# Spectral mixing and hash-routed experts: the loads of token blocks from the second on, issued by SyncE instead of ScalarE

## The chip, the cores and the metric

The kernel runs on one core of a Trainium2 chip. The metric is the device time of one execution in microseconds (us). The kernel before the change has a median of 1469.29 us over 14 runs (1464.46 to 1480.11). The engines are called PE (TensorE), DVE (VectorE), ACT (ScalarE), POOL (GpSimd) and SP (SyncE). SP does no arithmetic here: it loads registers and issues transfers. ACT copies and applies relu, and issues transfers as well.

## What is computed

The reference, cut to what matters:

```python
# x (8, 2496, 256); filt_r, filt_i (1249, 256)
X = np.fft.rfft(x, axis=1)
Y = X * (filt_r + 1j * filt_i)[None]
y = np.fft.irfft(Y, n=2496, axis=1).reshape(19968, 256)

expert = token_ids * 2654435761 % 8
for e in range(8):
    m = expert == e
    out[m] = np.maximum(y[m] @ w1[e], 0) @ w2[e]      # w1 (8, 256, 1024), w2 (8, 1024, 256)
```

Each of 8 batches goes through a filter in the frequency domain along its 2496 tokens. Then each of the 19968 tokens goes through the two-layer network of one of 8 experts, which its id chooses. All is in 32-bit floats.

## The kernel before

**The spectral part** splits 2496 into 39 x 64 and does each transform as two rounds of small matmuls with table matrices. For a batch there are four kinds of matmuls on PE: `pa` (first round forward, from tiles `x`), `pb` (second round forward, from `t2`, that is slots of the tile `mid`), then the product with the filter on DVE, `pc` (first round back) and `pd` (second round back, from tiles `t`). For batches 2 to 7 the turn of the data between two rounds goes through DRAM: ACT copies the result of `pa` and writes it to `d1` (L286, shown as `d<-mid`), SP reads it as `mid<-d` (L292, `load2`); ACT copies the result of `pc` and writes `d2` (L331, `d<-mid` too), SP reads it as `t<-d` (L395, `load4`). SP also loads the input (`x<-in_x_dram`, L239, `load1`). The finished rows, with their token number in column 256, are scattered by POOL (L414) to a DRAM table `xs`, in which all tokens of an expert lie together, in blocks of 256 rows.

**The expert part** is a loop of steps, one for each block of 256 rows of `xs`; 80 blocks are always worked, and up to 5 more under conditions. Step i is made of:

- `up(i)` (L850): the first layer, as seven products on halves of the matrices instead of eight, into the banks `up_a`, `up_b`, `up_c`. ACT copies the first product out (L861), DVE adds the others to it (L857, `plus`), ACT applies relu (L854). POOL prepares the sums of weights (`tw`, L840) for the step after, DVE the sums of tokens (`st`, L831).
- `down(i)` (L885): the second layer into `dps`; DVE copies it out (L890), POOL scatters the rows to the output (L977).
- From step 50 on `both(i)` takes the place of the two, with seven products in the second layer too (L907 and L912; the sums of `w2` for it, `t2s`, are prepared once and loaded by SP, L450).

**The loads of a step.** The two weight matrices (1 MB each) of block i + 2 are loaded by SP, L445 and L448, into the tile `wts`, which holds two pairs. They wait until PE has done with the pair of block i; when block i + 2 has the same expert as block i the issue is skipped. A block of tokens is loaded by `load(i)` (L807): four transfers of 64 rows each into the tile `xg` (two buffers), laid out so that DVE can transpose 32 x 32 squares (L818, `token_parts`), and one transfer of the 256 token numbers into the tile `no` (eight buffers). These five issues are what the change touches. Before, those of block 0 are shared (three by SP, two by ACT), those of block 1 are SP's, and those of all later blocks are ACT's.

**Where a block is asked for.** `ask(i)` calls `load` for the next block. In `up(i)` it stands after ACT's copy L861 (`between`), where it asks up to block i + 2; at the first quarter of `down(i)` (`spot`, k = 0) it may ask for block i + 3 if that block lies in the same stage as the one before. In `both(i)` it stands after the same copy and asks for block i + 2. A load waits until the transpose of the block two before has freed its buffer.

**Stages.** The spectral work of later batches runs between the steps: `todo` gives each of its pieces a place in units of steps, and `run_until` puts the pieces whose place has come into the program, after `up`, between the quarters of `down`, and after it. The blocks are ordered so that the first ten hold only tokens of batches 0 and 1, the next ten of batches up to 2, and so on (`STAGES = (2, 3, 4, 6, 8)`), so experts start while later batches are still being filtered. The first load of a stage therefore waits for the scatters of the batches that it adds.

**Order and waits.** Each engine works through its instructions in the order of the program; the order is by hand. Waits are put in by the framework. Transfers issued by SP and ACT share eight completion semaphores, and an issue waits until the last transfer that was given its semaphore has landed, whichever engine issued that one.

Of the kernel before, what the change touches and what calls it, by code (L numbers as in the profile page):

```python
# [119 lines left out]
def kernel(  # L120
# [10 lines left out]
    nc = tc.nc  # L131
# [625 lines left out]
    todo += [(-75.5, lambda: [nc.sync.dma_start(out=dram, in_=chip) for dram, chip in put_off])]  # L757
    todo += [(t, lambda k=k: weights(k // 2, k % 2)) for k, t in enumerate((-101, -98, -95, -92))]
    todo += [(-84.9, lambda: begin()), (-84.4, lambda: [load(i) for i in range(2)])]

    def batch(b, t1, t2, t3):
# [36 lines left out]
    def load(i):  # L798

        g = gath.tile([P, TB // 32, C // 4], F32, name=f"xg_{i}", tag="xg")  # L800
        no = nums.tile([P, 2], I32, name=f"no_{i}", tag="no")
        rows = xs[tiles[i] * TB:(tiles[i] + 1) * TB, :]
        moves = [(g[32 * q:32 * q + 32, :, :], rows[:, 64 * q:64 * q + 64].rearrange("(a t) c -> t a c", t=32))
                 for q in range(4)]
        moves.append((no[:].bitcast(F32), rows[:, C:C + 1].rearrange("(h p) c -> p (h c)", p=P)))
        for k, (to, src) in enumerate(moves):
            ld = (nc.sync if i < 2 and (i or k < 3) else nc.scalar).dma_start(out=to, in_=src)  # L807
            for b in range(STAGES[stage_of[i]], B):
                tc.declare_no_dep(ld.ins, group=f"xs_{b}", reason="the tiles of a stage hold tokens of its batches alone")
            if stage_of[i] < G - 1:  # L810
                tc.declare_no_dep(ld.ins, group="xs_pad", reason="places without a token lie in the last stage alone")
            tc.add_to_no_dep_group("xs_read", ld.ins)
        xg[i], to_rows[i] = g, no
# [177 lines left out]
    def ask(i, sooner=False):  # L991

        j = asked[0]
        if j <= i + 2 or (sooner and j == i + 3 < NT and stage_of[j] == stage_of[j - 1]):
            if j < NT:
                load(j)
                asked[0] += 1
# [48 lines left out]
    def rest(k):  # L1046
        with tc.If(used[0] > blocks[k][0]):
            for i in blocks[k]:
                ht = work.tile([P, 2, FP, P], F32, name=f"ht_{i}", tag="ht")
                if i >= NSURE + 2:  # L1050
                    for j in ((i, i + 1) if i == NSURE + 2 else (i + 1,)):
                        if j < NT:
                            load(j)
                    token_parts(i)
                token_sums(i)
                weight_sums(i, nc.vector)
                up(i, ht)
                weights(i + 2, 0)
                down(i, ht)
                store(i)  # L1060
                weights(i + 2, 1)
            if k + 1 < len(blocks):
                rest(k + 1)
# [30 lines left out]
```

## Time and profile before

| | |
|---|---|
| median of 14 runs | 1469.29 us (1464.46 to 1480.11) |
| profiled execution | 1468.48 us, its span 1466.7 us |
| mean granted PE clock | 0.979 |
| PE busy | 1395.8 us, 95% |
| ACT busy | 420.2 us, 29% |
| transfers issued by SP (q1) | 89087 packets, 169.76 MB |
| transfers issued by ACT (q10) | 131806 packets, 56.23 MB |
| transfers issued by POOL (q0) | 19920 packets, 44.59 MB |
| L807 on ACT | 321 issues of `xg`, median 462 ns; 81 of `no`, median 464 ns |
| L807 on SP | 7 issues of `xg`, median 448 ns; 1 of `no`, 452 ns |

Times count from the start of the span. The profile is of one execution, 0.81 us faster than the median of the runs. "Busy" leaves out issuing transfers, loading registers and waiting for semaphores, so ACT's and SP's time in L807 is in none of the shares. `ACTq` and `SPq` name the issue queues of ACT and SP. In a list of waits a line says who waited for whom, then the total in us, how often, and the longest. A wait for several semaphores is put down to the one that came last. Lines of a timeline give start, duration, engine, line of the code, operation, result and source, the number of instructions merged, and in brackets the idle time before with what ended it. The execution falls into three parts: up to about 153 us mostly spectral work and routing, from there to about 1075 us steps 0 to 49 mixed with the spectral work of batches 2 to 7, then steps 50 to 79, which last 12.5 us each.

### The profile page before, as it was taken

Reading aid. Unit: us, or ns where it says so; the run is one execution under the profiler, and the core shown is the slowest. Engines: PE = TensorE matmul, PEld = TensorE weight load, DVE = VectorE, ACT = ScalarE, POOL = GpSimd, SP = SyncE. Lnnn points to the kernel's source line nnn. Section 1 sums busy time; section 2 is a strip of 40 time slices with the busy share of each in tenths; the row PEclk is TensorE's granted clock in tenths of the full one; section 3 lists DMA queues with packets and bytes.
Section 4 is the critical chain, followed back from the end, with each engine's and each line's share of the span. In section 5 each row is a group of like instructions: output and inputs, shape, how many; then the busy total and the mean of one; then the engine's idle time right before and its main releaser. Section 6 shows DMA issues by size and latency. Waiting matters only on the chain.

```text
span 1466.7 us, 26476 instructions
## 1 busy us (share of the span) xinstructions
PE 1395.8 (95%) x9494; PEld 1293.4 (88%) x9494; DVE 871.7 (59%) x1641; ACT 420.2 (29%) x770; POOL 822.7 (56%) x732
## 2 busy tenths in 40 slices
PE   8988799899999989999999899999999999999997
PEld 7976688888988878888999899998999999999997
DVE  7862565366465546533766367744557767677765
ACT  4543122222223213223222222222222222222222
POOL 5066332763465464557535387878855555555553
PEclk9997899999999999999999999999999999999999
DMA  8236675667887597697764667688661616161611
GB/s 234 74 101 216 181 226 156 201 200 240 269 245 245 154 303 229 218 272 242 259 196 120 196 215 233 203 245 244 198 212 43 211 43 209 44 215 45 212 45 34
DMA packets 240947, 272.32 MB, mean 186 GB/s; under 512 B 124940, under 2 KB 210879, under 8 KB 231389
## 3 DMA queue, kind: packets, MB, share of 16 engines
q1 hardware_dynamic: 89087, 169.76, 37.1%
q10 hardware_dynamic: 131806, 56.23, 15.6%
q0 software_dynamic: 19920, 44.59, 8.7%
q8 instruction: 78, 1.28, 0.4%
q14 instruction: 56, 0.46, 0.1%
HBM read 290.24 MB, written 83.53 MB: 255 GB/s over the span
## 4 chain that ended last, share of the span: by engine, by line
PE 80%; DMA 9%; DVE 4%; issue 3%; another core or an unknown queue 1%; ACT 1%; POOL 1%; ACTq 1%; SPq 0%; POOLq 0%; DVEq 0%
PE dps L885 19%; PE up_b L850 8%; PE up_a L850 5%; PE up_c L850 5%; PE pd L257 4%; PE pb L301 4%; PE dnc L912 4%; PE dna L912 4%; PE dnb L912 4%; PE upc L907 4%; PE upa L907 4%; PE pa L257 3%; PE pc L324 3%; PE upe L907 2%; PE upg L907 2%
## 5 line engine op out<-in xcount | busy, mean ns | idle before, releaser
L885 PE MATMUL dps<-wts,ht 128*128 128x256 f32 x1600 | 367.4, 380 | 0.3 <-ACT ht L854 0.3
L885 PEld LDWEIGHTS dps<-wts,ht 128*128 128x128 f32 x1600 | 302.1, 190 | 43.9 <-ACT ht L854 1.3
L977 POOL DMA_INDIRECT out_dram<-osb,no x158 | 165.0, 1045 | 231.4 <-DVE osb L919 142.8
L414 POOL DMA_INDIRECT xs<-o,sidx x176 | 175.9, 1000 | 195.4 <-ACT o L259 78.2
L840 POOL TENSOR_TENSOR tw<-wts 128x512 f32<-128x512 f32 x158 | 204.8, 1297 | 110.7 <-DMA wts<-in_moe_w_dram 81.1
L840 POOL TENSOR_TENSOR tw<-wts,tw 128x512 f32<-128x512 f32 x158 | 205.7, 1302 | 6.2
L857 DVE TENSOR_TENSOR ht<-up_b,ht 128x512 f32<-128x512 f32 x150 | 103.7, 692 | 137.5 <-PE up_b L850 79.0
L854 ACT ACTIVATE ht<-ht 128x512 f32<-128x512 f32 x150 | 94.5, 630 | 201.7 <-DVE ht L857 174.7
L850 PE MATMUL up_a<-xt,wts 128*128 128x128 f32 x800 | 119.1, 283 | 23.8 <-ACT ht L861 11.9
L890 DVE COPY osb<-dps 128x512 f32<-128x512 f32 x50 | 34.6, 692 | 168.0 <-PE dps L885 122.5
L850 PEld LDWEIGHTS up_a<-xt,wts 128*128 128x128 f32 x800 | 108.8, 198 | 28.2 <-ACT ht L861 12.9
L311 DVE TENSOR_TENSOR z<-pb,filt 64x512 f32<-64x512 f32 x160 | 110.2, 689 | 38.0 <-PE pc L324 33.9
L850 PE MATMUL up_b<-st,tw 128*128 128x128 f32 x800 | 110.4, 282 | 4.3 <-DVE ht L857 3.3
L850 PEld LDWEIGHTS up_b<-st,tw 128*128 128x128 f32 x800 | 100.7, 197 | 6.7 <-issue 3.5
L857 DVE TENSOR_TENSOR ht<-up_c,ht 128x512 f32<-128x512 f32 x100 | 69.0, 690 | 46.0 <-PE up_c L850 30.5
L916 ACT ACTIVATE ht<-ht 128x512 f32<-128x512 f32 x90 | 56.8, 631 | 120.5 <-DVE ht L919 72.5
L257 PE MATMUL pd<-t,wi_t 120*117 120x256 f32 x320 | 79.0, 390 | 7.2 <-DVE t L387 5.0
L307 DVE TENSOR_TENSOR y<-pb,filt 128x512 f32<-128x512 f32 x80 | 55.2, 690 | 41.0 <-PE pb L301 26.6
L327 ACT COPY mid<-pc 128x512 f32<-128x512 f32 x60 | 35.0, 584 | 149.7 <-PE pc L324 90.0
L259 ACT COPY o<-pd 117x512 f32<-117x512 f32 x80 | 44.7, 586 | 111.3 <-DMA xg<-xs 41.6
L861 ACT COPY ht<-up_a 128x512 f32<-128x512 f32 x50 | 29.3, 587 | 163.4 <-PE up_a L850 98.7
L257 PEld LDWEIGHTS pd<-t,wi_t 120*117 120x117 f32 x320 | 58.0, 185 | 19.9 <-issue 6.1
(210 smaller groups left out, 2499.1 us busy)
## 6 DMA issues: line engine op xcount, KB each, us to landing
wts<-in_moe_w_dram SPq DMA_DIRECT2D x160, 1024.0 KB
xg<-xs ACTq DMA_DIRECT2D x321, 64.0 KB
mid<-d SPq DMA_DIRECT2D x60, 256.0 KB
d<-mid ACTq DMA_DIRECT2D x60, 256.0 KB
d_t<-t2s SPq DMA_DIRECT2D x15, 1024.0 KB
e_t<-t2s SPq DMA_DIRECT2D x15, 1024.0 KB
t<-d SPq DMA_DIRECT2D x12, 960.0 KB
x<-in_x_dram SPq DMA_DIRECT2D x36, 312.0 KB
```

The source lines that it names most:

```text
L257: nc.tensor.matmul(out=ps[0:cols * H, k, :], lhsT=w[:], rhs=src[:, 2 * i + k, :], start=True, stop=True)
L301: nc.tensor.matmul(out=ps[:, i, :], lhsT=d_t[:, s, :], rhs=rhs, start=True, stop=True)
L311: nc.vector.tensor_tensor(out=z[b], in0=ps[a], in1=f_t[1][64 * hi:64 * hi + 64, s1:s1 + 2, :], op=OP.mult)
L414: st = nc.gpsimd.indirect_dma_start(out=xs[:], out_offset=bass.IndirectOffsetOnAxis(ap=index, axis=0), in_=rows, in_offset=None, bounds_ch ...
L840: eng.tensor_tensor(t[k][:], p, q, op=OP.subtract)
L850: nc.tensor.matmul(out=ps[bank][:, f, :], lhsT=w[:, f * P:(f + 1) * P], rhs=xx, start=first and f == 0, stop=True, skip_group_check=True)
L854: nc.scalar.activation(out=out, in_=in_, func=AF.Relu)
L857: nc.vector.tensor_tensor(out, ps[bank][:], other, op=OP.add)
L885: nc.tensor.matmul(out=ps[:, h, :], lhsT=ht[:, h, fp, :], rhs=w2[:, fp, :], start=(fp == 0), stop=(fp == FP - 1))
L907: nc.tensor.matmul(out=ps[:, f, :], lhsT=w[:, f * P:(f + 1) * P], rhs=xx, start=first and f == 0, stop=True, skip_group_check=True)
L912: nc.tensor.matmul(out=ps[:, 0, :], lhsT=a[:, f, :], rhs=b[:, f, :], start=first and f == 0, stop=True, skip_group_check=True)
L977: st = nc.gpsimd.indirect_dma_start(out=out[:], out_offset=bass.IndirectOffsetOnAxis(ap=to_rows[i][:, h:h + 1], axis=0), in_=o[:, h, :], i ...
```

## The change

One line of `load` is changed:

```diff
         for k, (to, src) in enumerate(moves):
-            ld = (nc.sync if i < 2 and (i or k < 3) else nc.scalar).dma_start(out=to, in_=src)
+            ld = (nc.scalar if i == 0 and k >= 3 else nc.sync).dma_start(out=to, in_=src)
             for b in range(STAGES[stage_of[i]], B):
```

For block 0 the rule gives the same as before (k from 0 to 2 to SP, 3 and 4 to ACT), and for block 1 too (SP). From block 2 on all five transfers are issued by SP. What is transferred, and the place of the call in the program, stay the same; on SP the five issues now stand between the register loads, weights and spectral loads that surround the call. The framework gives the eight semaphores out anew for the changed program. The instructions of PE, DVE and POOL are the same, in the same order; ACT has 166 rows fewer in the list of the built program (956 before, 790 after, alike neighbours counted as one row), SP has 167 more (836 before, 1003 after).

## Prediction

> **What bounds the kernel now.** I read the page first, then the trace by stages, then TensorE's waits inside the stages, then the other engines around the longest waits. The page's span and engine row:
>
> ```profile
> span 1466.7 us, 26476 instructions
> PE 1395.8 (95%) x9494; PEld 1293.4 (88%) x9494; DVE 871.7 (59%) x1641; ACT 420.2 (29%) x770; POOL 822.7 (56%) x732
> ```
>
> PE is the bound: all its idle time is 1466.7 - 1395.8 = 71 us. ACT, from which the change takes work, is busy 29%, so only those of its delays count that reach PE. The table of stretches shows where they are. Its columns are stretch, length, busy us and count of PE, PEld, DVE, ACT and POOL, PE clock, DMA share, GB/s:
>
> ```profile
> 153.00:1075.00 922.00, 885.19 (x5327) 800.37 (x5326) 503.81 (x833) 247.08 (x440) 534.94 (x472) 0.98 0.73 220
> 1075.00:1467.00 392.00, 382.90 (x3394) 381.49 (x3392) 268.73 (x605) 106.24 (x212) 215.16 (x178) 1.00 0.38 115
> ...
> 419.00:426.00 7.00, 5.53 (x32) 5.37 (x33) 2.67 (x4) 2.69 (x6) 5.36 (x6) 0.76 0.90 226
> ...
> 828.00:835.00 7.00, 5.31 (x25) 5.31 (x26) 1.98 (x3) 1.70 (x3) 0.00 (x0) 0.52 0.33 110
> 175.00:183.00 8.00, 4.95 (x12) 3.90 (x13) 3.68 (x7) 1.17 (x2) 5.84 (x5) 0.58 0.44 122
> ```
>
> Up to 153 us the change moves nothing that runs (blocks 0 and 1 keep their engines). From 1075 us on (steps 50 to 79) PE has one wait of 0.6 us. The middle, 153 to 1075, has 922 - 885 = 37 us of PE idle, and after a gap the clock falls to about half for a few us: in the last three rows it is 0.76, 0.52 and 0.58, which is 0.24 x 7 = 1.7, 0.48 x 7 = 3.4 and 0.42 x 8 = 3.4 us lost besides the gap. PE's waits in the middle (total, times, longest):
>
> ```profile
> PE up_a L850 <- ACT ht L861: 11.9, 4, 3.9
> PE up_b L850 <- DVE ht L857: 6.1, 8, 1.9
> PE up_a L850 <- issue: 6.1, 2, 5.7
> PE pa L257 <- DMA x<-in_x_dram: 4.0, 1, 4.0
> PE pd L257 <- DMA t<-d: 2.2, 1, 2.2
> ```
>
> Two of the four waits for ACT's L861 copy come from the issues that the change moves. The larger, on ACT and then on PE:
>
> ```profile
> 817.83 3.99 ACTq L807 DMA_DIRECT2D xg<-xs  x4
> 828.63 0.38 ACTq L807 DMA_DIRECT2D no<-xs  x1
> 829.05 0.59 ACT L861 COPY ht<-up_a 128x512 f32<-128x512 f32 x1 [11.93 <-DMA xg<-xs]
> ```
>
> ```profile
> 829.69 0.58 PE L850 MATMUL up_a<-xt,wts 128*128 128x128 f32 x1 [3.71 <-ACT ht L861]
> ```
>
> Four parts of a block are issued, then ACT stands 6.8 us before the fifth (the numbers, `no`). The trace shows why: SP's and ACT's transfers share eight completion semaphores, and an issue waits until the last transfer on its semaphore has landed. Here that was a `d<-mid` issued at 816.89 and landed at 828.55. The copy that PE needs is queued behind. At 404.4 it is the same: the numbers wait until 418.2 for a 1 MB weight load (issued 403.70, landed 418.23), and PE loses 3.02 us at 420.36.
>
> **The change part by part.**
>
> *Removed from ACT.* Blocks 2 to 81 are loaded: 80 x 5 = 400 issues leave ACT. Their row:
>
> ```profile
> L807 ACTq DMA_DIRECT2D xg<-xs x321: 309/462/2860, 146.1 to 1448.3; - x161
> ```
>
> At a median 0.462 us this is 400 x 0.46 = 185 us of ACT's time; in the middle the 250 issues there hold ACT about 204 us with their waits. Of that only what ends a PE wait counts: 3.71 + 3.4 at 829 and 3.02 + 1.7 at 420, **-11.8 us**. The other two waits for L861 (283.5, 691.3) are not from these issues: ACT stood idle before the copy with nothing of L807 in hand. I leave those, and the 5.7 us "issue" wait at 547, where they are. At 829 the next thing late once ACT is free is DVE's `plus`, 0.7 us behind the copy, so nearly the whole gap goes.
>
> *Added to SP: issue time.* 400 x 0.46 us, 2.3 us a block. The built program puts a block on SP after the first weight load of a step (L445) and before the second (L448). SP waits there already:
>
> ```profile
> SPq L448 <- PE dps L885: 193.3, 31, 14.5
> ...
> SPq L445 <- PE up_c L850: 121.7, 32, 9.9
> ...
> SPq L448 <- DMA xg<-xs: 32.6, 5, 9.4
> ...
> SPq L292 <- DMA xg<-xs: 24.0, 6, 5.8
> ```
>
> 193.3 / 31 = 6.2 us a step, against 2.3. So the weights leave at the same time, and I cost the issues at nothing. Without that cover the weights would be 2.3 us later; `tw` is ready 6.7 us or more before the matmuls of its tile in every step of the middle (read tile by tile), so still nothing.
>
> *Added to SP: waits.* A moved issue still waits for its semaphore and for the transpose (L818) that frees its buffer; behind it on SP now stand weights, FFT loads and, at a stage's first block, the scatters' end. The last two rows above show that SP stood behind these blocks' landings already. The block itself has room: it lands 14.9 us or more before its transpose in the middle. In the last stage it is 8.3 us, but 2.5 to 3.0 us in the eight steps where weights are exchanged: a block issued at 1146.39 landed 9.2 us later and was transposed at 1158.53. There it now goes out behind 2 MB on SP's queue instead of beside them on ACT's. Both orders end with the same bytes moved, and t2's 1 MB landed 8.4 us after 1146.18, so I take up to 1 us later, inside 2.5: nothing.
>
> *FFT loads behind a block.* Here it can cost. Reading landing against first use for the loads of the FFT batches, three have no room: `t` of batch 2 (256.0), `t` of batch 3 (402.3), `x` of batch 3 (178, the 4.0 us wait); then `mid` of batches 4 and 5 with 2.2 and 3.5 us, `t` of batch 7 with 4.1; the next has 7.3. In the new order a block stands ahead of `t` of batch 3 and `mid` of batch 4, where none did: 2.3 us of issue each. Bounds: nothing, if the queue then moves `t` without the block beside it (its 960 KB took 13.3 us with block and `mid` beside it), to 2.3 + 3.4 us of clock for each, 11.4 us. For the waits of SP itself no row shows the new queue; they could take off 0, or add what ACT lost, 11.8. I take **+5 us**, nearer to the 2.3 us issue row than to the long waits.
>
> *Loads that gain.* At 153 to 174 us blocks 2 and 3 now go out after the second spectrum loads and the six `x` loads, not before: two times 256 KB less ahead of `x`, and eight issues no longer waiting for semaphores that blocks 2 and 3 held (`mid` at 167.19 waited for one landed at 167.18). The `x` issues ran 169.0 to 173.6; I estimate 167 or earlier, and up to 4.0 + 3.4 = 7.4 us gain. Against it: block 2 lands at some 177 then (it was 158.4), and its transpose was at 173.8, so DVE stands 3 us. I take half, **-3.7 us**.
>
> *Against a page.* A block of the last stage landed 9.2 us after its issue beside 2 MB of weights and 3.4 us alone. The Trainium skill's "DMA: Bandwidth & Descriptors" ("Issuing engines are not separate DMA queues") says that issuing from several engines only saves issue time, since all share the 16 DMA engines; the 9.2 us agrees, and by it the sum stands. The same page ("Queues, rings and completion order") says that SP and ACT each own a ring on each DMA engine, served in turn, and that one ring is consumed in order. This speaks against the change: a block would lose its turns and stand behind a whole megabyte. By that, 1 MB at the 220 GB/s of the table is 4.8 us later, 2.3 us over the room, eight times, an estimate of +18 us and some 1476.
>
> *Sum.* 1468.5 (the profiled execution, 1466.7 span plus 1.8 around it) - 11.8 + 5 - 3.7 = **1458**. The median of the 14 runs is 0.8 us above that execution, which I neglect.
>
> **The rivals.**
>
> *Slower.* SP becomes the place where everything stands in line: the first FFT loads of a batch come later by d behind the blocks' waits. For d = 4 the six tight loads cost 3 x 4 + 1.9 + 0.6 = 14.4 (the 4.1 us one nothing), plus three times 3.4 of clock, 24.6 - 11.8 = +13, or 1481; if the clock holds, 1471. It decides from d = 3.3 without the clock (9.9 + 1.2 = 11.1), from about 2.5 with it (the 2.2 us gap at 256 brought no fall of the clock, the 3.0 us one did). For it: SP waits for these landings already, up to 9.4 us. Against: SP stands idle for PE 6.2 us a step, just there.
>
> *No change.* ACT keeps 80 `d<-mid` issues, which wait on the same eight semaphores (up to 3.6 us today). If their predecessors, now on a later SP, land later, the 11.8 us come back in other steps: 1465 to 1473.
>
> *More.* Half and whole of the `x` gap, the 2.2 us at 256 and small gaps go, and nothing is added: 1468.5 - 11.8 - 7.4 - 2.2 = 1447.
>
> That the change does nothing it says is excluded: in the built program 400 issues change engine.
>
> **How the numbers follow.** Forecast 1452 to 1465: 0.42. More: 0.13. No change: 0.22. Slower: 0.23. 0.3% is 4.4 us, about what can be told from no change here; faster is then 0.55, within 0.22, slower 0.23. The range takes in the added costs up to 1480 and the gain to 1448; some 0.18 lies outside.
>
> **What would show it.** Right: no ACT wait of 4 us or more with L807, no PE gap at the places of 420 and 829, the middle at 910 us or less, L448's wait for PE smaller by about 2 us a step. Wrong: PE waits of 2 us or more for `t`, `mid` or `x`, or ACT standing before L331 and L286. The last stage should keep its 12.5 us a step; a late transpose there would show the page's order right.

## The result and the profile after

The changed kernel takes 1484.36 us (median of 10 runs, 1479.8 to 1491.09) against 1469.14 us of the kernel before on the same chip: a ratio of 1.0105, 95% interval 1.0080 to 1.0129. It is slower by 1%, where 1458 us was forecast. The profiled execution took 1491.44 us, some 7 us over the median, so that differences between the two pages are larger than the real one.

The page after, span and engines:

```profile
span 1489.7 us, 26536 instructions
PE 1404.4 (94%) x9494; PEld 1299.4 (87%) x9494; DVE 873.0 (59%) x1641; ACT 422.0 (28%) x770; POOL 823.0 (55%) x732
```

The two stretches behind the start, with the columns of the table of before:

```profile
153.00:1095.00 942.00, 891.66 (x5311) 804.28 (x5312) 506.74 (x837) 247.78 (x438) 533.85 (x473) 0.97 0.72 215
1095.00:1489.70 394.70, 385.62 (x3416) 384.03 (x3414) 270.80 (x606) 107.33 (x214) 216.07 (x180) 0.99 0.38 117
```

The first stretch is 20 us longer (922 before), the second 3 us, but the two cuts do not lie at the same point of a step. Counted exactly, the first `upa` matmul of step 50 starts at 1081.93 us before and at 1104.34 after, 22.4 us later, and from there to the end it is 384.8 and 385.4 us. So the place is the middle, where FFT batches run beside the experts. TensorE's waits in the middle (total, times, longest):

```profile
PE up_b L850 <- DVE ht L857: 13.1, 7, 4.7
PE pd L257 <- DMA t<-d: 10.6, 3, 6.0
PE up_a L850 <- ACT ht L861: 8.2, 3, 4.2
PE dps L885 <- DMA wts<-in_moe_w_dram: 6.6, 2, 4.4
```

The waits for `t` are up from 2.2 to 10.6 us, and the second layer (`dps`) waits for its weights, which it never did before. The gaps of before at 420 and 829 us behind ScalarE's issues are gone. SyncE's waits in the same stretch show where the loads became late:

```profile
SPq L807 <- DMA d<-mid: 114.8, 19, 12.6
SPq L445 <- PE up_c L850: 53.8, 19, 7.0
SPq L807 <- DMA wts<-in_moe_w_dram: 34.6, 13, 6.5
SPq L292 <- DMA d<-mid: 31.4, 5, 13.4
SPq L448 <- PE dps L885: 30.3, 10, 6.5
```

Before, SyncE waited 193.3 us for TensorE ahead of L448: it was early. That is now 30.3 us. In its place SyncE waits 114.8 us, ahead of the moved issues, for the stores `d<-mid`. A block's data has nothing to do with these stores (batch results on their way to DRAM, issued by ScalarE); the wait is for a shared completion semaphore. In all 19 waits of that row the issue stands on a semaphore whose last user was a store of ScalarE, and in 10 of them, 88 us of the 114.8, ScalarE had not yet issued this store when SyncE got there. A place of this kind (start, us, what; a group of several issues has its stands inside):

```profile
651.24 0.40 SPq L448 DMA_DIRECT2D wts<-in_moe_w_dram  x1
653.35 0.63 SPq L445 DMA_DIRECT2D wts<-in_moe_w_dram  x1
654.14 14.97 SPq L807 DMA_DIRECT2D xg<-xs  x4
669.22 0.39 SPq L807 DMA_DIRECT2D no<-xs  x1
669.70 0.92 SPq L395 DMA_DIRECT2D t<-d  x2
670.92 0.40 SPq L448 DMA_DIRECT2D wts<-in_moe_w_dram  x1
```

and on ScalarE in that time:

```profile
657.70 0.80 ACTq L286 DMA_DIRECT2D d<-mid  x2
```

Four issues that take 2 us take 15. The third stands on a semaphore whose user before it, eight places earlier in the program, is a store that ScalarE issues only at 657.70, after SyncE has come there at 655.57; the last landing that the trace has of this store is at 667.94, and the third issue goes out at 668.27. (Because of these 0.3 us the list of waits leaves this stand out, so that 114.8 us is not all.) `t` and the next weights stand behind. Between 155 and 1090 us the moved issues waited 238 us on SyncE, while the same ones waited 62.7 us on ScalarE, with every gap ahead of an issue counted (208 and 65 us by the rule of the wait lists). On ScalarE the stores stand ahead of the blocks on the same engine, so that they have always been issued when a block's turn comes; SyncE runs ahead of ScalarE, and by these waits it is held back to it.

Late weights also reach GpSimd, which makes weight sums from them in order with its scatters (group, busy and mean, idle before it and what ended it; the first line is of before, the second of after):

```profile
L840 POOL TENSOR_TENSOR tw<-wts 128x512 f32<-128x512 f32 x158 | 204.8, 1297 | 110.7 <-DMA wts<-in_moe_w_dram 81.1
L840 POOL TENSOR_TENSOR tw<-wts 128x512 f32<-128x512 f32 x158 | 203.6, 1289 | 193.5 <-DMA wts<-in_moe_w_dram 164.5
```

The idle time for weights has doubled. While GpSimd waits, the scatters of FFT results behind it pile up and then go out in rows: 8 or more in a row, 0.3 us apart, twice in the middle of before, four times after. Near these rows and a few looser ones TensorE, VectorE and ScalarE stand for up to 5 us and more; TensorE's gaps there add up to some 12 us before and 22 us after.

Adding up from the first matmul of `up` on: TensorE's gaps go from 36.2 to 48.5 us, the time lost to the half clock (an estimate: the length of the clock's records at 0.5, halved) from 19.4 to 29.3 us. With 3.2 us by which the first `up` starts later these are 25 us, against 23.0 of the spans: 2 us too many. Some records at half clock begin inside a gap (at 828.3 us in before, while the gap ends at 829.7), so that gap and half clock overlap there. The start is not the change's doing: it lay between 151 and 160 us in all kernels of this study on this kind of chip, unchanged ones among them. A second pair of traces on one chip gave 32.8 and 41.6 us of gaps, 20.6 and 23.8 us of clock, for 12.3 us of span.

### The profile page after: what moved, and what is told of

The parts are those of the page before. It is cut to its first block, busy times and chain, and to the rows that moved or that the text cites. A ratio compares the mean times of both kernels' runs of the same rounds, so it can differ in the third digit from the quotient of the medians.

```text
span 1489.7 us, 26536 instructions
## 1 busy us (share of the span) xinstructions
PE 1404.4 (94%) x9494; PEld 1299.4 (87%) x9494; DVE 873.0 (59%) x1641; ACT 422.0 (28%) x770; POOL 823.0 (55%) x732
## 4 chain that ended last, share of the span: by engine, by line
PE 78%; DMA 10%; DVE 4%; issue 2%; another core or an unknown queue 2%; SPq 2%; ACT 1%; ACTq 0%; POOLq 0%; POOL 0%; DVEq 0%
PE dps L885 19%; PE up_b L850 7%; PE up_c L850 5%; PE up_a L850 5%; PE pd L257 5%; PE dnc L912 4%; PE dna L912 4%; PE dnb L912 4%; PE pb L301 3%; PE upc L907 3%; PE upa L907 3%; PE pa L257 3%; PE pc L324 3%; DMA t<-d 2%
## 5 line engine op out<-in xcount | busy, mean ns | idle before, releaser
L885 PE MATMUL dps<-wts,ht 128*128 128x256 f32 x1600 | 371.3, 383 | 6.6 <-DMA wts<-in_moe_w_dram 6.6
L840 POOL TENSOR_TENSOR tw<-wts 128x512 f32<-128x512 f32 x158 | 203.6, 1289 | 193.5 <-DMA wts<-in_moe_w_dram 164.5
L840 POOL TENSOR_TENSOR tw<-wts,tw 128x512 f32<-128x512 f32 x158 | 204.5, 1294 | 6.2
L311 DVE TENSOR_TENSOR z<-pb,filt 64x512 f32<-64x512 f32 x160 | 110.2, 689 | 32.4 <-PE pc L324 30.3
L257 PE MATMUL pd<-t,wi_t 120*117 120x256 f32 x320 | 81.9, 400 | 15.3 <-DMA t<-d 10.6
L861 ACT COPY ht<-up_a 128x512 f32<-128x512 f32 x50 | 29.3, 586 | 172.6 <-PE up_a L850 120.4
```

Of the source, the lines that this page charges most:

```text
L257: nc.tensor.matmul(out=ps[0:cols * H, k, :], lhsT=w[:], rhs=src[:, 2 * i + k, :], start=True, stop=True)
L311: nc.vector.tensor_tensor(out=z[b], in0=ps[a], in1=f_t[1][64 * hi:64 * hi + 64, s1:s1 + 2, :], op=OP.mult)
L840: eng.tensor_tensor(t[k][:], p, q, op=OP.subtract)
L885: nc.tensor.matmul(out=ps[:, h, :], lhsT=ht[:, h, fp, :], rhs=w2[:, fp, :], start=(fp == 0), stop=(fp == FP - 1))
```

## The experiments

The 18 runs fell into groups in which the kernel before took 1466 to 1469 us, and groups in which it took 1431 to 1433, on other chips. Each ratio is against the kernel before in its own group.

| run | before, us | time, us | ratio, 95% interval |
|---|---|---|---|
| late_only | 1468.68 | 1468.06 | 0.9987, 0.9962 to 1.0013 |
| mid_only | 1468.68 | 1488.97 | 1.0117, 1.0083 to 1.0151 |
| block_after_w2 | 1468.68 | 1481.86 | 1.0076, 1.0049 to 1.0104 |
| first_act | 1468.68 | 1487.07 | 1.0094, 1.0058 to 1.0129 |
| numbers_sp | 1432.99 | 1424.00 | 0.9944, 0.9925 to 0.9963 |
| numbers_act | 1432.99 | 1439.74 | 1.0065, 1.0043 to 1.0088 |
| after_spaced | 1432.99 | 1462.48 | 1.0211, 1.0188 to 1.0235 |
| before_spaced | 1432.99 | 1467.75 | 1.0232, 1.0205 to 1.0259 |
| after_again | 1465.78 | 1481.34 | 1.0083, 1.0051 to 1.0114 |
| before_again | 1465.78 | 1467.52 | 1.0006, 0.9971 to 1.0041 |
| sp_busy | 1465.78 | 1461.86 | 0.9959, 0.9938 to 0.9980 |
| after_d_pool | 1465.78 | 1451.26 | 0.9878, 0.9848 to 0.9908 |
| before_d_pool | 1430.66 | 1426.09 | 0.9964, 0.9947 to 0.9980 |
| numbers_sp_again | 1430.66 | 1423.67 | 0.9956, 0.9934 to 0.9979 |
| numbers_sp_d_pool | 1430.66 | 1423.01 | 0.9949, 0.9928 to 0.9969 |
| after_d_pool_again | 1433.22 | 1425.44 | 0.9939, 0.9916 to 0.9961 |
| before_d_pool_again | 1433.22 | 1427.83 | 0.9966, 0.9943 to 0.9989 |
| after_third | 1433.22 | 1445.21 | 1.0073, 1.0045 to 1.0102 |

### Which blocks cost

```diff
# late_only
+            ld = (nc.sync if i >= 52 or i < 2 and (i or k < 3) else nc.scalar).dma_start(out=to, in_=src)
# mid_only
+            ld = (nc.sync if 2 <= i < 52 or i < 2 and (i or k < 3) else nc.scalar).dma_start(out=to, in_=src)
# first_act
+            ld = (nc.sync if i >= 4 or i < 2 and (i or k < 3) else nc.scalar).dma_start(out=to, in_=src)
```

late_only. 

> Blocks from the 53rd on (i >= 52) by SyncE, those of steps 0 to 49 by ScalarE as before. Theory (SP, which issues in order, is held by the moved issues' waits and issue time while the FFT batches run, so FFT loads and weights come late to TensorE): nothing lost, 0.998 to 1.002 of the time before, since the late steps have no FFT loads and showed 12.5 us per step in both traces. Rival A (the late steps lose, at the change of weights, behind the 1 MB tables): 1.005 or more. Rival B (ScalarE freed of 28 blocks gains): 0.997 or less.

mid_only. 

> Blocks 2 to 51 by SyncE, the later ones by ScalarE as before. Theory: the whole loss, 1.008 to 1.013, with SP's waits before L807 for d<-mid near 115 us and PE waits for t<-d near 11 us as in the changed kernel. Rival A (the late steps lose): 1.004 or less.

first_act. 

> As the changed kernel, but blocks 2 and 3 by ScalarE as before. Theory: only the stand at 188 us goes (TensorE 2.2 + 0.9 us and the half clock behind it), and the gain on x at 178 us may appear with it: 1.005 to 1.009. Rival E (most of the loss comes from the first steps, and all later differences follow from this shift): 1.003 or less.

The late blocks cost nothing (0.9987), the middle ones all of it (1.0117). In mid_only TensorE waited 10.0 us for `t` and 7.5 us for w2 weights, as in the changed kernel. In first_act the stand at 188 us is gone, but with 1.0094, just over the expected range, its effect can't be told from none; the first blocks are not the bulk of the loss.

### The place of the issues on SyncE

```diff
# block_after_w2: in spot()
-        if k == 0:
-            ask(i, True)
# in step(), behind the second weights
         weights(i + 2, 1)
+        ask(i, True)
         run_until(i + 1)
```

> All blocks from the third on by SyncE, but a block that may be asked for early is issued behind the w2 weights of its step instead of ahead of the FFT loads and of these weights. Theory (what stands behind the block's issues on SP is late): the waits of down for w2 weights (6.6 us in the changed kernel) and most of pd's for t (10.6 us) go, weight sums on POOL wait less, and with them some long scatter runs; 0.998 to 1.005. Rival C (blocks on the same ring as the weights delay these wherever they are issued): 1.007 or more, with w1 late instead. Rival D (SP's issue time and waits summed over a step are simply too long): 1.007 or more, waits moved to the next step's FFT loads.

The theory as it stood here (what stands behind the blocks on SyncE is late, so put them behind) missed with 1.0076. TensorE's wait for w2 did go, and that for `t` fell to 7.0 us, but SyncE stood just as long, now ahead of the first weights. Its waits in the middle:

```profile
SPq L807 <- DMA d<-mid: 127.7, 17, 14.3
...
SPq L445 <- DMA d<-mid: 34.8, 6, 13.1
```

GpSimd waited 182.1 us for weights (162.7 in the changed kernel, same stretch), and the gaps near rows of scatters stayed at some 20 us. Something is late behind the blocks wherever they stand. That fitted the theory of the waits as well as rival C, queueing on the ring (with w1 late instead), and rival D, too much load on SyncE.

### Load or waits

```diff
# sp_busy: kernel before, in load()
         xg[i], to_rows[i] = g, no
+        for _ in range(8 if 2 <= i < 52 else 0):
+            nc.sync.value_load(chunk_i[0:1, 0, 0:1], min_val=0, max_val=E - 1)
```

> The kernel before, with eight register loads added on SyncE in each of steps where blocks 2 to 51 are asked for: about 2.5 to 3 us of SyncE's time at the place where the changed kernel issues a block, as long as its five issues took (3.1 us per block), but with no wait on a DMA; the blocks stay on ScalarE. Theory (waits on the shared semaphores make SyncE late, not the time of the issues): 0.998 to 1.003. Rival D (SyncE's load in itself): 1.005 to 1.010, a large part of the loss.

The register loads took more than planned, 272 us in 50 steps or 5.4 us a step, against 3.1 us for the issues of a block. Even so nothing was lost; the kernel was 0.4% faster, more than the theory had said. That small gain is not explained. What changed with it: against before_again on the same chip, ScalarE's waits at L807 fell from 61 to 30 us by the rule of the wait lists, and TensorE's waits for L861 from 10.9 to 4.5 us. Had all of the 11.8 us that ScalarE's waits were to have cost come back, the load could hide some 8 us behind this gain, less than a third of the 27 us that the change added by the medians (a loss of 15 us with 11.8 us gained). SyncE's waits for TensorE shrank and took up the load:

```profile
SPq L448 <- PE dps L887: 112.4, 24, 10.3
SPq L445 <- PE up_c L852: 86.1, 25, 5.7
```

Rival D is out as the main cause: SyncE has the time.

### Which of the five issues

```diff
# numbers_sp
+            ld = (nc.sync if i >= 2 and k == 4 or i < 2 and (i or k < 3) else nc.scalar).dma_start(out=to, in_=src)
# numbers_act
+            ld = (nc.sync if i >= 2 and k < 4 or i < 2 and (i or k < 3) else nc.scalar).dma_start(out=to, in_=src)
```

numbers_sp. 

> As the kernel before, but the `no` issue of every block from the third on goes to SyncE; the four `xg` issues stay on ScalarE. In the trace of before ScalarE waited 62.7 us at L807 between 155 and 1090 us, 42.9 us of it at `no`. Theory (waits on shared semaphores, not the number of issues, decide): ScalarE's two long stands go, SyncE takes on at most 39 us of waits (what `no` cost it in the changed kernel) of its some 190 us of slack: 0.992 to 0.999. Rival D (SP's load decides, in proportion to issues): a fifth of the loss, 1.001 to 1.003.

numbers_act. 

> The reverse: the four `xg` issues of a block by SyncE, `no` by ScalarE as before. Theory: of SyncE's 238 us of waits at L807 199 us were at xg, so nearly the whole loss stays, 1.006 to 1.013, with TensorE waits for t and w2 as in the changed kernel. Rival F (`no`, with its 4-byte elements, is what holds SyncE or its ring): 1.003 or less.

numbers_sp_again. 

> `no` by SyncE and xg by ScalarE once more, beside the runs with the stores on GpSimd and, if the chip allows it, where the kernel before takes about 1469 us: 0.992 to 0.998 on each chip, with no stand of TensorE behind ScalarE's L807 above 2.5 us. Rival (its gain belonged to the other chip): 0.999 or more.

One issue in five on SyncE gains 0.56%, and 0.44% the second time; the other four lose 0.65%. So the loss doesn't go by the number of issues. With `no` alone moved SyncE waits 13 us in all at L807 between 155 and 1095 us, none of it for `d<-mid`, and TensorE has 8.6 us of gaps left from the first `up` on. This is the gain that the forecast was after, had with 80 issues in place of 400. Both runs were on chips where the kernel before takes 1431 to 1433 us; on the other kind this version was not run.

### Taking the stores off the shared semaphores

```diff
# after_d_pool: in stage1() and back(); before_d_pool: the same on the kernel before
-                    nc.scalar.dma_start(out=dram, in_=chip)
+                    (nc.gpsimd if self.b > 1 else nc.scalar).dma_start(out=dram, in_=chip)
...
-                    nc.scalar.dma_start(out=self.d2[:, a0:a0 + SG, :],
+                    (nc.gpsimd if self.b > 1 else nc.scalar).dma_start(out=self.d2[:, a0:a0 + SG, :],
```

after_d_pool. 

> The changed kernel, with the stores of FFT results d<-mid of batches 2 to 7 issued by GpSimd instead of ScalarE, whose DMAs have semaphores of their own. Theory: SyncE's waits at L807 for d<-mid (115 us in the changed kernel) fall below 25 us, and with them TensorE's waits for w2 (6.6 us) and most of those for t that came from late issues; the time itself may lose elsewhere, since GpSimd, in order, issues these stores behind scatters and weight sums: 0.993 to 1.010. Rival C (queueing on SyncE's ring): waits of TensorE for w2 and t stay as they are though SyncE's waits go.

before_d_pool. 

> The kernel before (all blocks from the third on by ScalarE) with the stores d<-mid of batches 2 to 7 issued by GpSimd, as in the run of the changed kernel with these stores. Theory (the change loses through SyncE's waits for these stores, and gains what ScalarE's waits at L807 cost): ScalarE's waits for the blocks' semaphores stay, 0.993 to 1.002, so that with the stores away the change itself gains 0.3 to 1.2%. Rival H (the whole gain of 1.2% comes from moving the stores, whoever issues the blocks): 0.984 to 0.991.

The blocks stay on SyncE, with all their issues, on the same ring as weights and FFT loads; only the stores change engine. SyncE's longest waits in after_d_pool:

```profile
SPq L448 <- PE dps L885: 138.0, 29, 11.0
SPq L445 <- PE up_c L850: 107.0, 31, 6.9
SPq L807 <- DVE st L831: 40.9, 25, 2.4
```

No wait for `d<-mid` is left at L807, SyncE is early again, GpSimd's idle time ahead of L840 is 42.0 us instead of 193.5, the wait of TensorE for w2 is gone, that for `t` 2.8 us. The kernel is 1.2% faster than before, more than its expected range had it. Rival C falls with it: the ring is as full as it was.

The last three runs put both kernels and both places of the stores on one chip.

after_d_pool_again. 

> Blocks by SyncE, stores d<-mid of batches 2 to 7 by GpSimd, once more, on one chip with the kernel before with these stores and with the changed kernel. Theory: faster than the kernel before with the stores moved by 0.2% or more (0.983 to 0.994 of before). Rival H: the same as that kernel within 0.2%.

before_d_pool_again. 

> Blocks by ScalarE, stores by GpSimd: 0.994 to 0.999 of before, as in the run before this one.

after_third. 

> The changed kernel. Theory: 1.003 to 1.008 where before takes about 1430 us, 1.008 to 1.013 where it takes about 1466; so 1.2 to 2.3% slower than with the stores by GpSimd.

| blocks by | stores by ScalarE | stores by GpSimd |
|---|---|---|
| ScalarE | 1 | 0.9966 (0.9943 to 0.9989) |
| SyncE | 1.0073 (1.0045 to 1.0102) | 0.9939 (0.9916 to 0.9961) |

With the stores on ScalarE the change loses 0.7%; with the stores away the loss is gone, and it is 0.3% ahead by the ratios, which the intervals don't separate from nothing. SyncE's wait at the blocks in after_third is

```profile
SPq L807 <- DMA d<-mid: 125.9, 22, 12.3
```

and after_d_pool_again has none of it. The same on TensorE: its waits in after_third,

```profile
PE pd L257 <- DMA t<-d: 11.4, 3, 5.9
PE dps L885 <- DMA wts<-in_moe_w_dram: 4.7, 2, 4.5
```

and in after_d_pool_again:

```profile
PE up_b L850 <- DVE ht L857: 3.2, 3, 2.2
PE pa L257 <- DVE z L311: 2.4, 2, 1.8
PE pd L257 <- DMA t<-d: 2.1, 1, 2.1
```

Gaps and lost clock from the first `up` on are 23.2 + 13.1 us in the first and 8.2 + 10.2 us in the second: 17.9 us, against 19.6 us by which that part of the span is longer. What these runs leave open: moving the stores takes them off ScalarE and off its ring as well as off the semaphores, and each edit makes the framework hand the semaphores out anew. The wait that went is one for a semaphore, since a block needs no data of these stores, and before_d_pool_again shows what the move of the stores brings where SyncE doesn't issue the blocks (0.9966); but no run moved the semaphores alone.

numbers_sp_d_pool. 

> Both together: `no` by SyncE, xg by ScalarE, the stores d<-mid of batches 2 to 7 by GpSimd. Theory: between the kernel before and the changed kernel with the stores on GpSimd, or like the latter: 0.984 to 0.993. Rival H: 0.984 to 0.991 like the two others with these stores.

Both edits together give 0.9949, short of the range expected (0.984 to 0.993) and not clearly more than either one. Several versions beat both kernels: blocks by SyncE with stores by GpSimd (0.9878 and 0.9939 on two chips), and `no` alone by SyncE (0.9944 and 0.9956, both where before takes 1431 to 1433 us), the smaller edit.

### Rows of scatters

```diff
# after_spaced, before_spaced: in stage3(), from batch 2 on
                 scatter(o[0:r, i, :], sidx[0:r, self.b, j:j + 1], f"xs_{self.b}")
+                if self.b > 1 and i % 2 == 1:
+                    for _ in range(5):
+                        nc.gpsimd.memset(space[:], 0.0)
```

after_spaced. 

> The changed kernel with five small memsets on GpSimd (about 1 us) after every second scatter of FFT results from batch 2 on, so that long rows of scatters are broken up. Theory of a second step (late weights bunch the scatters, and long rows of them make TensorE, VectorE and ScalarE stand): the stands near long rows (22.5 us in the changed kernel, and some 10 us of half clock behind them) fall to 10 us or less: 0.994 to 1.005. Rival G (the rows of scatters only happen to lie there): 1.008 to 1.018.

before_spaced. 

> The kernel before with the same memsets. Theory of the second step: stands near long rows fall from 11.5 us to 5 us or less: 0.990 to 0.998. Rival G: 0.999 to 1.008 (GpSimd has 45% idle time, but its weight sums come later).

Both became some 2% slower, outside both expectations: with 65 us of memsets on GpSimd the weight sums are late, and TensorE waits 16.1 us for them in the kernel before. And this chip has no stand to remove: numbers_sp, on the same chip, has rows of 10, 8 and 10 scatters at 260, 513 and 642 us without a gap of TensorE near them. So the question was not answered, and it changed: the rows alone do not make the engines stand.

after_again. 

> The changed kernel once more, beside the kernel before on a chip on which its trace is taken too (the last four runs were on a chip where the kernel before took 1433 us instead of 1469, and rows of 8 to 10 scatters had no stand of TensorE near them). Theory: the part that comes from late FFT loads and w2 weights (about 10 us net of what ScalarE gains) is there on each chip, the part near rows of scatters only on a chip that shows such stands: 1.008 to 1.013 where before takes about 1469, 1.003 to 1.008 where it takes about 1433. Rival: 1.0105 on both.

before_again. 

> The kernel before, unchanged, for its trace on this chip: 0.998 to 1.002. TensorE's gaps behind L807 on ScalarE (3.7 and 3.0 us) are there on each chip; stands near rows of scatters only if before takes about 1469.

Where before takes 1466 us, rows of 8 to 10 had gaps again (3.7 us at 691, and 2.1 and 1.7 us at 279 to 283 in after_again). In after_third, where it takes 1433, four rows of 8 to 10 between 250 and 700 us had none. The change lost 1.05% and 0.83% on the first kind of chip and 0.73% on the second. These intervals overlap, so that it isn't shown that the rows add to the loss; most of it is there without them.

## Why the prediction was wrong, step by step

*ScalarE's issues, -11.8 us: right in kind.* Both gaps are gone, and numbers_sp shows a gain of about 0.5% when little is put against it, 9.0 and 7.0 us in its two runs. The kernel before has no trace from those chips, so that the size of 11.8 us itself isn't shown; 0.7 us of it was counted twice, since the half clock at 828.3 us began 1.4 us before the gap ended.

*SyncE's issue time, nothing: right.* sp_busy put 5.4 us a step there without a loss. The cover of 6.2 us a step was misread, though: 193.3 us in 31 waits are 6.2 us a wait, and over the some 50 steps of the middle 3.9 us a step; and a block's issues took 3.1 us instead of 2.3.

*SyncE's waits, between 0 and 11.8 us, within the +5 us: wrong, and this is the step that failed.* The prediction saw the eight shared semaphores and the waits on them, and took as upper bound what ScalarE had lost by its waits. But a wait on a shared semaphore depends on who issues: what ScalarE had lost by its waits is no upper bound for SyncE. The moved issues waited 62.7 us on ScalarE and 238 us on SyncE, 4.8 us a block. With the 3.1 us of issues that is 7.9 us a step, more than either figure of the cover ahead of L448, and single waits are up to 13 us long. The cost on TensorE was not 5 us: from the two sums above, gaps and clock after minus before are 22.2 us in the first pair of traces and 12.0 us in the second, after the 11.8 us gained. So the added cost was some 24 to 34 us, an estimate that takes the 11.8 us for gained.

*Weights, nothing: wrong, by the same step.* The cover held for issue time, not for waits: w2 was issued late and waited for, 6.6 us.

*FFT loads: the right loads, too small.* `t` of batch 3 landed at 409.07 instead of 402.27 (3.2 us of it the later start), and TensorE waited 3.1 us for it; `t` of batch 7, which was given 4.1 us of room, made TensorE wait 6.0 us.

*`x` and block 2, -3.7 us: nothing came of it.* The `x` issues, estimated at 167 us or earlier, went out from 169.13 to 173.73, about as before (169.04 to 173.62). DVE stood 5.1 us for block 2 (3 were named), and TensorE lost 2.2 and 0.9 us at 188 to 191 us in place of the 4.0 us at 178.

*The last stage, nothing: right,* by late_only. The estimate of 1476 us from the Trainium skill's "DMA: Bandwidth & Descriptors" ("Queues, rings and completion order"), a block late behind a whole megabyte of its ring, did not come about: in the eight steps of the last stage with new weights a block landed 8.3 to 9.7 us after its first issue in the changed kernel, against 8.5 to 10.1 before, by the landings in the traces. The same page ("Issuing engines are not separate DMA queues") says that issuing on several engines saves only the time to initiate, usually small; sp_busy agrees in so far as 5.4 us a step of such time cost nothing here, and the stores' runs show that it was not what the change cost.

The rival "Slower" had the mechanism, first loads late behind the blocks' waits, with 1471 to 1481 us. It was given 0.23 because SyncE stood idle for TensorE; that idle time was there only as long as SyncE's own issues didn't have to wait for ScalarE.

## What to carry to other kernels

Where DMAs of several engines share a few completion semaphores, moving an issue moves its wait: look up whose transfer last used its semaphore in program order, and when that will be issued and landed at the moment the new engine gets there. An engine that runs ahead (here SyncE, the loader) loses its lead as soon as its issues share semaphores with late issues of an engine that it runs ahead of (here ScalarE's stores). Idle time of a queue covered the issue time here (sp_busy), not such waits; and moving the one issue that waits most (80 of 400 here) may give the whole gain.

## What the runs showed of the hardware

On chips where the kernel before took 1466 to 1469 us, TensorE, VectorE and ScalarE stood some 2 to 6 us near many rows of 8 or more scatters; where it took 1431 to 1433 us, rows as long left no gap of TensorE in numbers_sp and after_third. The cause of the stand, and of the 2.4% between the chips, is open. Behind many gaps of the middle TensorE's granted clock is at 0.5 for 3.41, 6.83 or 10.24 us, a multiple of the same 3.41 us each time: by estimate, half of the part that lies behind the gap is lost, up to 1.7, 3.4 or 5.1 us more than the gap's length.
